# Pooled attention with a routed feed-forward: the product for x one half later, the fetch of rows behind the next row sums, the totals ahead of the transposes

## The chip, the cores and the metric
The kernel runs on one core of one Trainium2 chip. The metric is the device time of one execution in microseconds, the median of several runs. A core has five engines that run their own instruction streams side by side and wait for each other by semaphores: TensorE (PE, matrix products), VectorE (DVE), ScalarE (ACT), GpSimd (POOL) and SyncE (SP), which here only issues DMAs. Times within a profile count from the start of the profiled execution.

## The reference
Two blocks, one behind the other, on float32 data (8 batches, 8 heads, 1152 positions, head size 64).

```
q_pool = q.reshape(B, H, S // 2, 2, D).mean(axis=3)        # 576 queries
scores = (q_pool @ k.transpose) / sqrt(D)
attn   = softmax(scores)                                   # exps / (sum + 1e-9)
x      = (attn @ v) -> (B, 576, 512)                       # heads side by side

gate   = x @ w_gate                                        # one score per row
for each batch: top = the 128 rows with the largest gate
    ye      = relu(x[top] @ w1) @ w2                       # 512 -> 1024 -> 512
    out[top] = x[top] + sigmoid(gate[top]) * ye
the other rows of out are x
```

The softmax is taken without the maximum, since the inputs are small; a second version of the kernel behind a test at the end covers other inputs and is not run here.

## The kernel before
**Tiling.** Two heads make a *pair*, and there are 4 pairs in a batch, 32 in all. The 576 queries of a pair are split in two *halves* of 288, so the main loop of `run` has 64 halves and one closing round. A half h with h even (s == 0) is the first of its pair.

**One round h of the loop.** TensorE computes `scores` of half h: nine chunks of 128 keys, each an own PSUM tile (L818), and ScalarE takes the exps of each chunk into `p` (L825). Then TensorE computes `weighted` of the half before, the product of exps and values (L836). ScalarE copies it from PSUM to `two` (L844), GpSimd adds its two halves to `av` (L846), VectorE transposes that in blocks to `avb` (L915). All PSUM tiles come from one pool of four; `p` has two buffers. The loop is in the order in which each engine executes; nothing moves instructions afterwards. What stands earlier in the text of a round stands earlier on its engine, and an instruction that waits holds all behind it on the same engine.

**Row sums.** `folded` (L857, L862, L872) adds up the exps: GpSimd adds chunks 0 to 2 to chunks 3 to 5 in three instructions (`acc`), VectorE folds both `acc` and chunks 6 to 8. For the two halves of a pair this gives `sum`. Two rounds later ScalarE brings the four blocks of partitions side by side (`groups`, L887), VectorE adds them (`total`, L893, in `added`), and in the next round ScalarE spreads the result over the partitions (`sums`, L902). `normalized` takes the reciprocal on VectorE (`rec`, L954), and GpSimd multiplies `avb` by it to get `x` (L956), which `stored` writes to DRAM by SyncE a round later (L968).

**Gate.** `multiplied` (GpSimd, `prod`, L925) and `gated` (VectorE, L979, L981) compute each row's gate score from `avb` and `rec`.

**The feed-forward of a batch** is a generator, `routed`. It is cut into pieces by `yield`; `units` runs each open batch's next piece. A piece marked "mid" runs between a round's scores and its weighted product, all others at the end of the round. The pieces in order: the gate scores go by way of DRAM to a row and to columns; VectorE ranks each row by counting (L1083 to L1102); the ranks go by DRAM to all partitions (`lines`); VectorE searches each slot's row number and its gate (`pick`, L1166); GpSimd adds the batch's offset to make `index` (L1175) and fetches 128 rows of x from DRAM by an indirect DMA (`xe`, L1183). In later rounds TensorE transposes these rows (L1197), multiplies by w1 (L1208) and by w2 (L1221), and GpSimd adds the result to the rows (L1245) and scatters them (L1246). The last three batches differ: batch 5's second product is kept for the end of the kernel, and batches 6 and 7 have only pieces for the end of a round or behind the loop. Batch 7 gets its scores spread by a product with `diag` (L1044, L1054).

**The order of a round** on the engines other than TensorE: exps; the four copies of `groups` (even h) or `sums` (odd h) on ScalarE; pieces marked mid; `gated`; `folded`; `multiplied`; for even h `prepare_pair` (GpSimd adds pairs of queries, `qp`, L732; VectorE transposes `kT`, L735, and `qT`, L739); `weighted` and `drained`; `total` for even h; `rec` and `x` for odd h; the other pieces.

Of the kernel before, what the change touches and what calls it, by code (L numbers as in the profile page):

```python
# [10 lines left out]
P = 128  # L11
BLK = 32

G = 3
F32 = mybir.dt.float32
# [519 lines left out]
class _Plain:  # L535
# [396 lines left out]
    def normalized(self, pair):  # L932

        nc, hp = self.nc, pair["hp"]
        tot = self.sums[:, pair["b"] * self.NPAIR + hp, :]
        if self.last_pair(pair):
            ps = self.banks()[:, 0, :]
            nc.tensor.matmul(
                ps[:, 0 : 2 * self.QB],
                lhsT=self.merge.rearrange("p g j -> p (g j)"),  # L940
                rhs=pair["sum"].rearrange("p j n -> p (j n)"),
                start=True,
                stop=True,
            )
            for j in range(2):
                rows = slice(j * self.D, (j + 1) * self.D)
                nc.scalar.activation(
                    tot[rows, :],
                    ps[rows, j * self.QB : (j + 1) * self.QB],
                    AF.Identity,  # L950
                    bias=self.tiny[rows, 0:1],
                )
        rec = pair["rec"] = self.small.tile([P, self.QB], F32, name="rec")
        nc.vector.reciprocal(rec[:, :], tot)  # L954
        x = self.work.tile([P, self.QB, BLK], F32, name="x")
        nc.gpsimd.tensor_tensor(  # L956
            out=x[:, :, :],
            in0=pair["avb"][:, :, :],
            in1=rec[:, :].unsqueeze(2).broadcast_to([P, self.QB, BLK]),
            op=ALU.mult,  # L960
        )
        pair["x"] = x

    def stored(self, pair):

# [7 lines left out]
    def gated(self, half):  # L973

        nc, pair, hb = self.nc, half["pair"], self.HB
        if half["s"] == 0:
            pair["red"] = self.small.tile([P, self.QB], F32, name="red")
        ns = slice(half["s"] * hb, (half["s"] + 1) * hb)
        nc.vector.tensor_reduce(pair["red"][:, ns], pair["prod"][:, ns, :], AX.X, ALU.add)  # L979
        if half["s"] == 1:  # L980
            nc.vector.tensor_tensor(  # L981
                out=pair["part"][:, pair["hp"], :],
                in0=pair["red"][:, :],
                in1=pair["rec"][:, :],
                op=ALU.mult,
            )
            if pair["hp"] == self.NPAIR - 1:
                unit = self.routed(pair["b"], pair["part"])
                at = next(unit) == "mid"
                self.routing.append([pair["b"], unit, at])  # L990

# [3 lines left out]
    def routed(self, b, part):  # L997


        nc, ffn, Sp, NT, NF = self.nc, self.ffn, self.Sp, self.NT, self.NF  # L1000
        tiles = [(t, P if t < NF else self.TAIL) for t in range(NT)]
        mid = "mid" if b < self.B - 2 else True
# [8 lines left out]
        if b < self.B - 1:  # L1011

            yield mid
            if b < self.B - 2:
                groups = self.side_by_side(line)
                yield True
                total = self.added(groups)
            else:
                total = self.small.tile([BLK, self.QB], F32, name="total")
# [117 lines left out]
        for s0, w in self.slots:  # L1137
# [3 lines left out]
            if b == self.B - 1:  # L1141

                nc.vector.tensor_tensor(
                    out=pick[:, :, 0:w],
                    in0=self.slot_f[:, s0 : s0 + w].unsqueeze(1).broadcast_to([P, NT, w]),
                    in1=rank[:, :].unsqueeze(2).broadcast_to([P, NT, w]),
                    op=ALU.is_equal,
                )
                yield True
                ps = self.banks()[:, 0, 0:2]  # L1150
                for t, rows in tiles:
                    nc.tensor.matmul(
                        ps[0:w, :],
                        lhsT=pick[0:rows, t, 0:w],
                        rhs=meta[0:rows, t, :],
                        start=(t == 0),
                        stop=(t == NT - 1),
                    )
                nc.scalar.copy(index[0:w, :], ps[0:w, 0:1])
                nc.scalar.copy(own_gate[0:w, :], ps[0:w, 1:2])  # L1160
            else:
                yield True

                found = self.small.tile([P, 1], F32, name="found_token")
                for of, to in ((self.token_line, found), (lines[:, :, 1, :], own_gate)):
                    nc.vector.scalar_tensor_tensor(  # L1166
                        out=pick.rearrange("p t i -> p (t i)").rearrange("p (i t) -> p i t", t=NT)[0:w],
                        in0=lines[0:w, :, 0, :],
                        scalar=self.token[0:w, s0 // P : s0 // P + 1],
                        in1=of[0:w, :, :],  # L1170
                        op0=ALU.is_equal,
                        op1=ALU.mult,
                        accum_out=to[0:w, :],
                    )
                nc.gpsimd.tensor_scalar(  # L1175
                    out=index[0:w, :],
                    in0=found[0:w, :],
                    scalar1=float(b * Sp),
                    scalar2=None,
                    op0=ALU.add,  # L1180
                )
            xe = ffn.tile([P, self.Dm], F32, name="xe")
            nc.gpsimd.indirect_dma_start(  # L1183
                out=xe[0:w, :],
# [3 lines left out]
                bounds_check=(b + 1) * Sp - 1,  # L1188
                oob_is_err=False,
            )  # L1190
            yield True
            yield mid

            xeT = ffn.tile([P, self.ND, P], F32, name="xeT")
# [95 lines left out]
        )  # L1290
        return count_i

    def units(self, mid):


        for entry in self.routing[::-1]:
            b, unit, at = entry
            if b in self.waiting or at != mid:
                continue
            end = next((mark for mark in unit if mark), None)  # L1300
            if end is None:
                self.routing.remove(entry)
            elif end == "hidden" and b == self.B - 3:
                self.waiting.add(b)
            entry[2] = end in ("mid", "hidden") and b < self.B - 2

    def run(self):
        nc = self.nc
# [13 lines left out]
        for h in range(n_halves + 1):  # L1322
            if h < n_halves:
                n, s = divmod(h, 2)
                if s == 0:
                    pair = upcoming
                    if pair["hp"] == 0:
                        part = self.ffn.tile([P, self.NPAIR, self.QB], F32, name="part")
                    pair["part"] = part
                else:  # L1330
                    loaded = None
                    if n + 2 < len(pairs):
                        loaded = self.load_pair(*pairs[n + 2])
                        self.load_values(loaded)
                    if n > 1:
                        self.stored(halves[h - 4]["pair"])
                if h > 1:
                    next(weights, None)
                half = {"pair": pair, "s": s}
                halves.append(half)  # L1340
                self.scores(half)
                if h > 1:

                    of = halves[h - 2 - s]["pair"]
                    if s == 0:
                        of["groups"] = self.side_by_side(of["sum"].rearrange("p j n -> p (j n)"))
                    else:
                        self.spread(of)
                self.units(mid=True)
                if h > 2:  # L1350
                    self.gated(halves[h - 3])
                self.folded(half)
                if h > 1:
                    self.multiplied(halves[h - 2])
                if s == 0 and loaded:
                    upcoming = loaded
                    self.prepare_pair(upcoming)
            else:
                self.stored(halves[h - 3]["pair"])
                self.gated(halves[h - 3])  # L1360
                self.multiplied(halves[h - 2])
                self.units(mid=True)
                self.units(mid=False)
            if h > 0:
                done = halves[h - 1]
                self.weighted(done)
                self.drained(done)
            if h == n_halves:
                self.multiplied(done)
                self.gated(halves[h - 2])  # L1370
            if 1 < h < n_halves and s == 0:
                done["pair"]["total"] = self.added(done["pair"]["groups"])
            if h == n_halves:
                self.normalized(done["pair"])
            elif h > 2 and s == 1:
                self.normalized(halves[h - 2]["pair"])
            if h < n_halves:
                self.units(mid=False)
        for _ in weights:
            pass  # L1380

# [90 lines left out]
```

## Time and profile before
The time is 708.08 us, the median of three runs (707.3 to 708.53). The profiled execution took 706.64 us, 704.8 of them between its first and last instruction.

| engine | busy us | share |
| --- | --- | --- |
| TensorE, products | 694.4 | 99% |
| VectorE | 496.5 | 70% |
| GpSimd | 485.1 | 69% |
| ScalarE | 444.5 | 63% |

| group | count | mean ns |
| --- | --- | --- |
| `acc`, GpSimd L857 | 192 | 1417 |
| `x`, GpSimd L956 | 32 | 1159 |
| `index`, GpSimd L1175 | 7 | 920 |
| fetch of `xe`, GpSimd L1183 | 8 | 1140 |
| fold, VectorE L862 | 128 | 1963 |
| `total`, VectorE L893 | 37 | 325 |
| search, VectorE L1166 | 14 | 873 |

How to read it: a row of a list of groups gives line, engine, operation, output<-inputs, shapes and count, then busy time and mean duration, then the idle time of the engine just ahead and who ended it. A line of the chain in order of time has its start, its length and what it is. A line of a timeline has start, length, engine, line, operation and count, and in brackets the idle time ahead of it with the instruction that ended it. A line of the list of waits says who waited for whom: the sum in us, how often, the longest. An engine that is not the bound may be idle without any loss.

### The profile page before, as it was taken

Reading aid. Unit: us, or ns where it says so; the run is one execution under the profiler, and the core shown is the slowest. Engines: PE = TensorE matmul, PEld = TensorE weight load, DVE = VectorE, ACT = ScalarE, POOL = GpSimd, SP = SyncE. Lnnn points to the kernel's source line nnn. Section 1 sums busy time; section 2 is a strip of 40 time slices with the busy share of each in tenths; the row PEclk is TensorE's granted clock in tenths of the full one; section 3 lists DMA queues with packets and bytes.
Section 4 is the critical chain, followed back from the end, with each engine's and each line's share of the span. In section 5 each row is a group of like instructions: output and inputs, shape, how many; then the busy total and the mean of one; then the engine's idle time right before and its main releaser. Section 6 shows DMA issues by size and latency. Waiting matters only on the chain.

```text
span 704.8 us, 23397 instructions
## 1 busy us (share of the span) xinstructions
PE 694.4 (99%) x9948; PEld 516.8 (73%) x9948; DVE 496.5 (70%) x793; ACT 444.5 (63%) x963; POOL 485.1 (69%) x452
## 2 busy tenths in 40 slices
PE   8999999999999999999999999999999999999996
PEld 5668899996758866688656887578775787766573
DVE  3877777996559965498754988559774697689540
ACT  6677778777547775477746776467754777477210
POOL 5877777868658695586955779467874877686520
PEclk9999999999999999999999999999999999999999
DMA  8888887858486483756928468382775728432200
GB/s 175 172 178 180 171 166 137 146 116 161 85 149 111 85 162 75 145 97 111 172 40 159 81 129 160 66 148 61 161 130 85 135 56 169 83 72 62 45 31 35
DMA packets 389490, 82.86 MB, mean 118 GB/s; under 512 B 376640, under 2 KB 376640, under 8 KB 389376
## 3 DMA queue, kind: packets, MB, share of 16 engines
q1 hardware_dynamic: 387872, 76.49, 58.1%
q0 software_dynamic: 1280, 4.20, 1.8%
q8 instruction: 80, 1.31, 0.8%
q10 hardware_dynamic: 224, 0.59, 0.3%
q14 instruction: 34, 0.28, 0.1%
HBM read 69.65 MB, written 11.59 MB: 115 GB/s over the span
## 4 chain that ended last, share of the span: by engine, by line
PE 89%; POOL 5%; issue 2%; DMA 1%; ACT 1%; DVE 1%; SPq 0%; POOLq 0%; DVEq 0%; ACTq 0%
PE ps L836 36%; PE ps L818 36%; PE ps L1208 8%; PE ps L1221 7%; POOL acc L857 2%; ACT p L825 1%; DMA kb<-in_k_dram 1%; DMA xe<-out_dram,index 1%; PE ps L1197 1%; POOL prod L925 1%; POOL x L956 0%; POOL av L846 0%; DVE fold L862 0%; POOL index L1175 0%; SPq L759 0%
## 5 line engine op out<-in xcount | busy, mean ns | idle before, releaser
L825 ACT ACTIVATE p<-ps 128x576 f32<-128x576 f32 x576 | 320.2, 695 | 1.7 <-PE ps L818 1.3
L818 PE MATMUL ps<-qT,kT 64*64 64x288 f32 x4608 | 295.2, 404 | 0.2 <-ACT p L825 0.2
L836 PE MATMUL ps<-p,v_sb 64*64 64x288 f32 x4608 | 294.6, 403 | 0.0
L857 POOL TENSOR_TENSOR acc<-p 128x576 f32<-128x576 f32 x192 | 266.3, 1417 | 15.4 <-ACT p L825 15.1
L836 PEld LDWEIGHTS ps<-p,v_sb 64*64 64x64 f32 x4608 | 215.5, 133 | 65.3 <-ACT p L825 9.2
L818 PEld LDWEIGHTS ps<-qT,kT 64*64 64x64 f32 x4608 | 208.0, 132 | 73.0 <-ACT p L825 15.4
L862 DVE TRANSPOSE_TENSOR_REDUCE fold<-p 128x54 f32<-128x1728 f32 x64 | 126.0, 1969 | 50.2 <-ACT p L825 50.2
L862 DVE TRANSPOSE_TENSOR_REDUCE fold<-acc 128x54 f32<-128x1728 f32 x64 | 125.3, 1957 | 46.0 <-POOL acc L857 45.8
L844 ACT COPY two<-ps 128x576 f32<-128x576 f32 x64 | 40.9, 639 | 156.9 <-PE ps L836 143.8
L846 POOL TENSOR_TENSOR av<-two 128x288 f32<-128x288 f32 x64 | 51.2, 800 | 96.5 <-ACT two L844 94.9
L915 DVE STREAM_TRANSPOSE avb<-av 128x288 f32<-128x288 f32 x64 | 29.4, 460 | 66.5 <-POOL av L846 66.5
L956 POOL TENSOR_TENSOR x<-avb,rec 128x576 f32<-128x576 f32 x32 | 37.1, 1159 | 40.3 <-DVE rec L954 27.9
L1208 PEld LDWEIGHTS ps<-xeT,w 128*128 128x128 f32 x512 | 57.8, 192 | 2.7 <-ACT p L825 2.6
L1208 PE MATMUL ps<-xeT,w 128*128 128x128 f32 x512 | 59.3, 277 | 0.0
L1221 PE MATMUL ps<-w,hT 128*128 128x512 f32 x128 | 57.3, 598 | 0.0
L925 POOL TENSOR_TENSOR prod<-avb,w_gate 128x288 f32<-128x288 f32 x64 | 51.5, 805 | 0.6 <-DVE avb L915 0.6
L902 ACT ACTIVATE sums<-total,tiny 32x18 f32<-32x18 f32 x124 | 38.1, 308 | 15.9 <-DVE total L893 14.2
L732 POOL TENSOR_TENSOR qp<-qb 128x576 f32<-128x576 f32 x31 | 43.8, 1414 | 2.2 <-DMA qb<-in_q_dram 2.2
L1221 PEld LDWEIGHTS ps<-w,hT 128*128 128x128 f32 x128 | 23.6, 190 | 28.1 <-issue 25.8
L735 DVE STREAM_TRANSPOSE kT<-kb 128x1152 f32<-128x1152 f32 x31 | 42.5, 1370 | 0.0
L887 ACT COPY groups<-sum 32x36 f32<-32x36 f32 x124 | 27.1, 219 | 6.7 <-DVE sum L872 5.2
L981 DVE TENSOR_TENSOR part<-red,rec 128x18 f32<-128x18 f32 x32 | 27.0, 845 | 1.1
(95 smaller groups left out, 290.6 us busy)
## 6 DMA issues: line engine op xcount, KB each, us to landing
kb<-in_k_dram SPq DMA_DIRECT2D x124, 144.0 KB
qb<-in_q_dram SPq DMA_DIRECT2D x124, 144.0 KB
v_sb<-in_v_dram SPq DMA_DIRECT2D x124, 144.0 KB
out_dram<-x SPq DMA_DIRECT2D x128, 72.0 KB
lines<-row_rank SPq DMA_DIRECT2D x7, 640.0 KB
w<-in_moe_w_dram SPq DMA_DIRECT2D x8, 512.0 KB
sc_row<-row SPq DMA_DIRECT2D x7, 288.0 KB
acc<-in_q_dram ACTq DMA_DIRECT2D x2, 288.0 KB
```

Of the source, the lines that this page charges most:

```text
L732: nc.gpsimd.tensor_tensor(out=qp[:, :, :], in0=pair["q"][:, :, 0, :], in1=pair["q"][:, :, 1, :], op=ALU.add)
L735: nc.vector.transpose(kT.rearrange("p (c g i) -> p c g i", c=self.NC, i=BLK), pair["k"].rearrange("p (g c) d -> p c g d", c=self.NC),)
L818: nc.tensor.matmul(sc[keys, j, 0:n], lhsT=pair["kT"][rows, c * P + keys.start : c * P + keys.stop], rhs=pair["qT"][rows, qs], start=True, ...
L825: nc.scalar.activation(p[:, c // G, c % G, :, :], sc[:, :, 0:n], AF.Exp, scale=self.scale)
L836: nc.tensor.matmul(av[j * self.D : (j + 1) * self.D, e, 0:n], lhsT=half["pair"]["v"][keys, j, c, :], rhs=half["p"][keys, c // G, c % G, j, :],
L844: nc.scalar.copy(two[:, :, :], av[:, :, 0:n])
L846: nc.gpsimd.tensor_tensor(out=half["av"][:, :], in0=two[:, 0, :], in1=two[:, 1, :], op=ALU.add)
L857: nc.gpsimd.tensor_tensor(out=acc[:, u, :], in0=units[:, 0, u, :], in1=units[:, 1, u, :], op=ALU.add)
L862: nc.vector.tensor_reduce(fold[:, a, :], of.rearrange("p u (m d) -> p (u m) d", d=BLK), AX.X, ALU.add, apply_transpose=True,)
L925: self.nc.gpsimd.tensor_tensor(out=pair["prod"][:, ns, :], in0=pair["avb"][:, ns, :], in1=self.w_gate[:, hp : hp + 1, :].broadcast_to([P, ...
L1208: nc.tensor.matmul(pv[:, f, 0:w], lhsT=self.w1[:, c, (f0 + f) * P : (f0 + f + 1) * P], rhs=xeT[:, c, 0:w], start=(c == 0), stop=(c == self ...
L1221: nc.tensor.matmul(ps[0:w, 0 : self.Dm], lhsT=hT[:, f, 0:w], rhs=self.w2[:, f, :], start=(f == 0), stop=(f == self.NFC - 1),)
```

## The change
- **x one half later.** The product for `x` moves out of `normalized` into a function of its own, `divided`, which runs a round later, at the end of the even round. It is meant to keep GpSimd from waiting for the reciprocal, which VectorE finishes at the end of the odd round. The last two pairs keep their place.
- **The fetch behind the next row sums.** `index` is made by VectorE, right behind the search. For batches 0 to 5 the fetch becomes a piece with the mark "sums", which runs in the next round, just behind that round's `folded`. It is meant to keep GpSimd from waiting for the search ahead of the row sums.
- **The totals.** `total` moves from behind the weighted product to just behind `multiplied`, ahead of `prepare_pair`'s transposes on VectorE.
- **The closing round.** There the pieces of open batches run behind the last weighted product instead of ahead of it.

```diff
-        rec = pair["rec"] = self.small.tile([P, self.QB], F32, name="rec")
-        nc.vector.reciprocal(rec[:, :], tot)
-        x = self.work.tile([P, self.QB, BLK], F32, name="x")
-        nc.gpsimd.tensor_tensor(
+        pair["rec"] = self.small.tile([P, self.QB], F32, name="rec")
+        nc.vector.reciprocal(pair["rec"][:, :], tot)
+
+    def divided(self, pair):
+
+        x = pair["x"] = self.work.tile([P, self.QB, BLK], F32, name="x")
+        self.nc.gpsimd.tensor_tensor(
             out=x[:, :, :],
             in0=pair["avb"][:, :, :],
-            in1=rec[:, :].unsqueeze(2).broadcast_to([P, self.QB, BLK]),
+            in1=pair["rec"][:, :].unsqueeze(2).broadcast_to([P, self.QB, BLK]),
             op=ALU.mult,
         )
-        pair["x"] = x
...
-                nc.gpsimd.tensor_scalar(
+                nc.vector.tensor_scalar(
                     out=index[0:w, :],
                     in0=found[0:w, :],
...
+                if b < self.B - 2:
+
+                    yield "sums"
             xe = ffn.tile([P, self.Dm], F32, name="xe")
             nc.gpsimd.indirect_dma_start(
...
-            yield True
+            if b >= self.B - 2:
+                yield True
             yield mid
...
-            entry[2] = end in ("mid", "hidden") and b < self.B - 2
+            entry[2] = self.place(b, end)
+
+    def place(self, b, mark):
+        if mark in (True, None) or b >= self.B - 2:
+            return "end"
+        return "mid" if mark == "hidden" else mark
...
-                self.units(mid=True)
+                self.units("mid")
                 if h > 2:
                     self.gated(halves[h - 3])
                 self.folded(half)
+                self.units("sums")
                 if h > 1:
                     self.multiplied(halves[h - 2])
+                if 1 < h and s == 0:
+                    last = halves[h - 1]["pair"]
+                    last["total"] = self.added(last["groups"])
                 if s == 0 and loaded:
                     upcoming = loaded
                     self.prepare_pair(upcoming)
...
-                self.units(mid=True)
-                self.units(mid=False)
             if h > 0:
                 done = halves[h - 1]
                 self.weighted(done)
                 self.drained(done)
             if h == n_halves:
+                for at in ("mid", "sums", "end"):
+                    self.units(at)
                 self.multiplied(done)
                 self.gated(halves[h - 2])
-            if 1 < h < n_halves and s == 0:
-                done["pair"]["total"] = self.added(done["pair"]["groups"])
             if h == n_halves:
                 self.normalized(done["pair"])
+                self.divided(done["pair"])
             elif h > 2 and s == 1:
                 self.normalized(halves[h - 2]["pair"])
+
+            if h == n_halves - 1:
+                self.divided(halves[h - 2]["pair"])
+            elif 3 < h < n_halves and s == 0:
+                self.divided(halves[h - 3]["pair"])
             if h < n_halves:
-                self.units(mid=False)
+                self.units("end")
```

More of the change, by code (lines that the diff above doesn't have):

```diff
@@ L988, in gated @@
                 unit = self.routed(pair["b"], pair["part"])
-                at = next(unit) == "mid"
-                self.routing.append([pair["b"], unit, at])
+                self.routing.append([pair["b"], unit, self.place(pair["b"], next(unit))])
     def banks(self):
@@ L1291, in outside, with units @@
         return count_i
-    def units(self, mid):
+    def units(self, at):
         for entry in self.routing[::-1]:
-            b, unit, at = entry
-            if b in self.waiting or at != mid:
+            b, unit, place = entry
+            if b in self.waiting or place != at:
                 continue
```

## The prediction
> **What bounds the kernel now.** I read the page's busy shares first:
> ```profile
> PE 694.4 (99%) x9948; PEld 516.8 (73%) x9948; DVE 496.5 (70%) x793; ACT 444.5 (63%) x963; POOL 485.1 (69%) x452
> ```
> TensorE is busy 694.4 of 704.8 us. No product is removed, so all there is to win lies in its holes. Of the 10.4 us without a product 2.1 lie before the first scores and 6.6 behind the last product (698.2), both outside the change; 1.7 are in between. Busy time is a record of starts, so TensorE can also lose time inside it. Next I read the chain of work in order of time, around the feed-forward of batch 2 (half 34 begins at 333.32):
> ```profile
> 328.94 4.38 PE ps L836 x72
> 333.32 4.62 PE ps L818 x72
> 337.94 0.59 PE ps L1197 x4
> 338.53 4.52 PE ps L836 x72
> 343.05 4.37 PE ps L818 x72
> 347.42 7.34 PE ps L1208 x64
> ```
> A half's scores (L818) take 4.37 us everywhere, except in the half whose scores are followed by the transposes of the fetched rows (L1197). From the start of these scores to the transposes, the six batches 0 to 5 take 4.47, 4.55, 4.62, 5.05, 4.61 and 4.98 us. Less 4.37 each, that is 0.10 + 0.18 + 0.25 + 0.68 + 0.24 + 0.61 = **2.06 us**, the only loss that repeats. The timeline of GpSimd and of ScalarE tells why; first GpSimd:
> ```profile
> 316.71 0.80 POOL L846 TENSOR_TENSOR av<-two 128x288 f32<-128x288 f32 x1 [1.52 <-ACT two L844]
> 319.63 1.16 POOL L956 TENSOR_TENSOR x<-avb,rec 128x576 f32<-128x576 f32 x1 [2.12 <-DVE rec L954]
> 321.09 4.14 POOL L857 TENSOR_TENSOR acc<-p 128x576 f32<-128x576 f32 x3
> 327.33 0.79 POOL L846 TENSOR_TENSOR av<-two 128x288 f32<-128x288 f32 x1
> 331.08 0.92 POOL L1175 TENSOR_SCALAR index<-found_token 128x1 int32<-128x1 f32 x1 [2.97 <-DVE pick L1166]
> 332.28 1.13 POOL L1183 DMA_INDIRECT xe<-out_dram,index  x1 [0.28 <-POOL index L1175]
> 333.44 4.14 POOL L857 TENSOR_TENSOR acc<-p 128x576 f32<-128x576 f32 x3
> ```
> x waits 2.12 for the reciprocals, so the row sums (acc) of half 32 begin late, and av at 327.33 instead of just behind its input (ScalarE's copy `two` ended at 325.31). Then GpSimd waits 2.97 for the search of the rows on VectorE, and only then fetches; the fetch lands at 337.33, against the transposes at 337.94. The row sums of half 33 come last. On ScalarE:
> ```profile
> 333.81 0.64 ACT L844 COPY two<-ps 128x576 f32<-128x576 f32 x1 [2.31 <-PE ps L818]
> ```
> TensorE's product was done at 333.32, by its record, but the copy starts at 333.81, elsewhere 0.1 us after it. In batches 0, 1, 2, 4 and 5 this signal comes 0.1 to 0.4 us after the fetch instruction has ended (here 333.41), so I read it as held up while GpSimd writes the fetch's descriptors. The exps then start late, a PSUM tile comes free late, and the transposes wait. In batch 3 the fetch started a microsecond later (419.02) and landed at 423.90, just ahead of the transposes at 424.04. The list of waits gives the sums over the run:
> ```profile
> POOL x L956 <- DVE rec L954: 27.9, 17, 3.2
> POOL index L1175 <- DVE pick L1166: 20.2, 7, 3.0
> ACT sums L902 <- DVE total L893: 14.2, 7, 2.8
> ```
> None of the three is time of TensorE by itself: they are what the change goes at. Last, the end of TensorE's timeline:
> ```profile
> 648.00 4.59 PE L836 MATMUL ps<-p,v_sb 64*64 64x288 f32 x72
> 653.20 0.63 PE L1197 MATMUL ps<-ident,xe 128*128 128x128 f32 x4 [0.61 <-DMA xe<-out_dram,index]
> 653.76 4.59 PE L836 MATMUL ps<-p,v_sb 64*64 64x288 f32 x72
> 658.53 5.40 PE L1221 MATMUL ps<-w,hT 128*128 128x512 f32 x12
> 664.28 1.21 PE L1054 MATMUL ps<-diag,ones 128*128 128x288 f32 x4 [0.35 <-DVE rank_parts L1076]
> ```
> Two plain holes: 0.61 us for batch 6's fetched rows and 0.35 for `diag` (its signal is counted with the memset behind it).
>
> **What the Trainium skill says.** "Perfetto Trace Analysis", the section on the per-instruction lifecycle: a matmul's end in the profile is an estimate, and the end of a DMA that GpSimd issues is when its descriptors are written, not when data lands. The trace agrees: the product estimated to end at 333.32 was signalled near 333.75, and the fetch that "ends" at 333.41 landed at 337.33. "DMA: Bandwidth & Descriptors", section "Anatomy of one DMA — SWDGE (gpsimd) path": about 2.0 us plus bytes/436e3, which for 128 rows of 2 KB would be an estimate of 2.6 us. Here they took 3.4 to 5.8 us from the start of the instruction, beside the loads, so I use the trace. "GPSIMD Engine Reference", section "Engine selection": elementwise work is better on VectorE. The trace agrees for the index: 0.92 us on GpSimd for one column, where VectorE's tensor_scalar of one element (L1283) takes 0.14.
>
> **The change part by part.** I carry the times of batch 2 through.
>
> (1) x later. At the end of half 32 GpSimd no longer waits for the reciprocals: after av (to 317.5) it has only the small gate op (0.24) ahead of the row sums. These need the exps of chunk 3 of the half; ScalarE started at 316.47 and takes 5.00 for nine, so chunk 3 is ready near 318.8. Three sums of 1.38: 318.8 to 322.9, where they ran 321.09 to 325.2. With prod 0.80 and qp 1.41 GpSimd is free at 325.1, av follows its input, 325.4 to 326.1, and x, now here, takes 1.16: 327.3. Its load per pair stays, but the even half carries 4.14 + 0.80 + 1.41 + 0.80 + 1.16 = 8.3 us of the 8.74 that TensorE gives a half, the odd one 5.7. It fits, without much room; what would be late is row sums, and p's two buffers give them another half.
>
> (2) Fetch behind the next row sums. The exps of half 33 start at 325.20, chunk 3 is ready at 327.5, so the sums run 327.5 to 331.65. The instruction starts near **331.75**, 0.5 us ahead of before, if the index is there.
>
> (3) Index on VectorE, total ahead of the transposes. VectorE loses two waits: 0.27 for the gate op and 0.85 for acc, in front of the fold at 325.26. The second search, which ended at 331.9, ends near 330.8. The index comes behind it: lower end 0.14 (L1283), upper end 0.92 as on GpSimd; I take 0.17, since VectorE's other ops of a few columns take 0.13 to 0.19. Ready at 331.0, or 331.7 at the upper end: no wait at either. The total costs the same 0.33 in its new place; its input, ScalarE's groups, has been ready 3 us. kT is finished 0.33 later, more than 8 us ahead of its scores. ScalarE's wait of 14.2 us over 7 places goes; behind it stand `two` and the next exps, which in these halves still waited for TensorE, so this is worth nothing by itself.
>
> (4) What TensorE gets. The fetch instruction now runs 331.75 to 332.9; with the 0.3 that the signal was held after it, 333.2, just before the signal of 333.32. The rows land 3.4 to 5.8 later, 335.2 to 337.6; the transposes want them at 333.32 + 4.37 = 337.69. So both causes of the 2.06 us go, narrowly. I count five sixths: **1.7 us**.
>
> (5) The end. Batch 6's transposes move behind the last weighted product: the hole of 0.61 is filled with 4.5 us of products. `diag` must come earlier too. GpSimd's sums of half 62 no longer stand behind x (638.85 to 640.0) and end near 642.4 instead of 644.44; VectorE's fold then has no wait (0.84), nor the 0.27 of the gate. The index comes at 648.2 and not 649.3, the fetch starts at 648.4 and not 649.57, and the last row sums, fold, sum, rec, x, prod and diag move with it, by 1.2 us, from 664.2 to 663.0. TensorE gets there at 664.28 - 0.35 - 0.61 = 663.3. Gain 0.61 + 0.35 = **0.96 us**. After that TensorE has work without a gap to the last product. Moving the scatters behind x (1.16 us) changes no wait of over 0.05 us.
>
> Sum: 1.7 + 0.96 = 2.7; 708.08 - 2.7 = **705.4 us**.
>
> **The rivals.** *Hidden anyway:* the fetch starts only 0.5 us earlier, the signal is still caught by it, and landings scatter by 2.4 us. Then only the end counts: 708.08 - 0.96 = 707.1, no measurable change. For it: the margins of step 4 are 0.1 us. Against: both only improve. *Slower, the fetch behind late sums:* the fetch is now queued behind three ops of 1.4 us that themselves wait for exps. If GpSimd runs 1.5 us later than in step 2, the rows land a microsecond after TensorE wants them, in six batches: 708.08 + 6 - 0.96 = 713; were the sums to end as late as before (337.6), it would be 6 x 4.8 = 29 us more, 736. Against: what made them late, the waits for rec and for the search, is what goes. *Slightly slower, GpSimd's even half:* 8.3 of 8.74 us leaves 0.4, and the feed-forward's add and scatter (1.28 + 1.05) come on top; if exps then wait for p by 0.3 us in 6 places, 708.08 + 1.8 - 0.96 = 708.9. Against: these stand in halves that the feed-forward's products lengthen by 7 us.
>
> **How the numbers follow.** Forecast 0.62, hidden 0.20, late fetch 0.11, full even half 0.07. The forecast's own spread is 703.9 (all 3.0 us, and about as much again as the timed runs lie above the profiled 706.64) to 706.6; with the hidden case and part of the slow ones the range is 703.9 to 708.4. Faster by over 0.2% (under 706.66): nearly all of the forecast and a little of the hidden case, 0.65. Slower by over 0.2%: 0.16. Within: 0.19.
>
> **What would show it.** Right: fetches start about 1.6 us ahead of the end of the product in front, with index in VectorE's rows at under 0.2 us; no wait of x for rec and of sums for total; L1197 4.4 us behind the start of its scores; no hole at 653; L1054 near one microsecond earlier, relative to the last scores. Wrong: L1197 waiting for the DMA of xe, or acc of the half before the transposes ending after their scores began.

## The result, and the profile after
The changed kernel takes **716.15 us**, the median of six runs (714.05 to 719.2), against 707.44 for the kernel before (705.75 to 708.53). The ratio is 1.0125, with a 95% interval of 1.0096 to 1.0153. It is slower, and outside the predicted range of 703.9 to 708.4.

The profiled execution spans 712.5 us, 7.6 more than before. The busy shares of its page:
```profile
PE 692.8 (97%) x9948; PEld 526.7 (74%) x9948; DVE 494.4 (69%) x800; ACT 443.2 (62%) x963; POOL 481.7 (68%) x445
```
Apart from TensorE's weight loads (PEld, 516.8 us before), no engine is busy for longer than before. TensorE has the same products and longer holes. What TensorE waited for, from the list of waits (sum, times, longest):
```profile
PE ps L1202 <- DMA xe<-out_dram,index: 5.5, 4, 1.8
PE ps L1202 <- ACT p L825: 1.5, 2, 0.8
PE ps L1055 <- DVE rank_parts L1077: 1.3, 1, 1.3
```
L1202 is the transposes of the fetched rows (L1197 before). They now wait for the rows themselves. Around batch 2, GpSimd's timeline; all times here lie 0.87 us later than before, since half 34 starts at 333.93 instead of 333.06:
```profile
319.77 4.15 POOL L857 TENSOR_TENSOR acc<-p 128x576 f32<-128x576 f32 x3 [1.07 <-ACT p L825]
...
327.01 1.16 POOL L959 TENSOR_TENSOR x<-avb,rec 128x576 f32<-128x576 f32 x1
328.50 4.74 POOL L857 TENSOR_TENSOR acc<-p 128x576 f32<-128x576 f32 x3 [0.34 <-ACT p L825]
334.27 1.13 POOL L1187 DMA_INDIRECT xe<-out_dram,index  x1 [1.03 <-DVE index L1176]
```
and VectorE's, with the two searches and the index:
```profile
330.62 1.35 DVE L1167 SCALAR_TENSOR_TENSOR pick<-lines,token,token_line 128x640 f32<-128x640 f32 x1
...
332.01 1.90 DVE L1167 SCALAR_TENSOR_TENSOR pick<-lines,token 128x640 f32<-128x640 f32 x1
...
333.85 0.14 DVE L1176 TENSOR_SCALAR index<-found_token 128x1 int32<-128x1 f32 x1
```
Before, VectorE's timeline had them at
```profile
330.13 0.86 DVE L1166 SCALAR_TENSOR_TENSOR pick<-lines,token,token_line 128x640 f32<-128x640 f32 x1
...
331.03 0.89 DVE L1166 SCALAR_TENSOR_TENSOR pick<-lines,token 128x640 f32<-128x640 f32 x1
```
while GpSimd stood waiting for them. Now they lie beside the row sums and take 1.35 and 1.90, and three sums that take 4.15 elsewhere take 4.74. GpSimd still waits for the index, 1.03 us, only behind the sums now. So the fetch starts later, not earlier. The start of the transposes in the six batches, counted from the start of their scores, both in TensorE's timeline (this gives some 0.2 us more than the chain of waits that the prediction counted in; 4.55 is the least that any run shows, so I take 4.55 to 4.58 for no hole; e6 and e13 are experiments told below):

| | b0 | b1 | b2 | b3 | b4 | b5 |
| --- | --- | --- | --- | --- | --- | --- |
| before | 4.68 | 4.74 | 4.81 | 5.33 | 4.80 | 5.22 |
| after | 5.38 | 5.38 | 6.42 | 6.17 | 5.11 | 6.36 |
| e6 | 4.57 | 4.56 | 4.56 | 4.56 | 4.56 | 4.56 |
| e13 | 4.57 | 4.56 | 4.56 | 4.58 | 4.56 | 5.41 |

From before to after these add up to 5.2 us. The end, in TensorE's timeline:
```profile
652.72 8.96 PE L836 MATMUL ps<-p,v_sb 64*64 64x288 f32 x144
661.61 0.66 PE L1202 MATMUL ps<-ident,xe 128*128 128x128 f32 x4
...
669.61 1.21 PE L1055 MATMUL ps<-diag,ones 128*128 128x288 f32 x4 [1.29 <-DVE rank_parts L1077]
```
The hole of 0.61 us at the transposes is filled, but the product with `diag` waits 1.29 instead of 0.35. It comes 21.25 us behind the start of the last scores, before 20.64: 0.6 us lost. Last, the program ends 8.76 us behind the start of VectorE's last operation on the fetched rows (`xe`), before 6.46: 2.3 us lost. The three terms, 5.2 + 0.6 + 2.3 = 8.1, less the 0.4 us by which the first scores start earlier in this profile (8.31 against 8.73), cover the 7.6.

The spread of the six runs goes with the granted TensorE clock: three with a mean of 0.996 or 0.997, the profiled one (714.2) among them, took 714.05 to 715.62 us, and three with 0.992 took 716.69 to 719.2.

### The profile page after: what moved, and what is told of

It is laid out like the page before. It is cut to its first block, busy times and chain, and to the rows that moved or that the text cites. A ratio compares the mean times of both kernels' runs of the same rounds, so it can differ in the third digit from the quotient of the medians.

```text
span 712.5 us, 23370 instructions
## 1 busy us (share of the span) xinstructions
PE 692.8 (97%) x9948; PEld 526.7 (74%) x9948; DVE 494.4 (69%) x800; ACT 443.2 (62%) x963; POOL 481.7 (68%) x445
## 4 chain that ended last, share of the span: by engine, by line
PE 65%; DVE 13%; DMA 7%; POOL 6%; issue 5%; ACT 3%; SPq 0%; POOLq 0%; DVEq 0%; ACTq 0%
PE ps L836 27%; PE ps L818 23%; PE ps L1213 8%; PE ps L1226 5%; DVE fold L862 5%; POOL acc L857 3%; DMA xe<-out_dram,index 3%; ACT p L825 2%; DMA lines<-row_rank 2%; DVE kT L735 1%; DVE tie L1103 1%; DVE cmp L1093 1%; DVE cmp L1084 1%; DMA row_rank<-both 1%; DVE pick L1167 1%
## 5 line engine op out<-in xcount | busy, mean ns | idle before, releaser
L818 PEld LDWEIGHTS ps<-qT,kT 64*64 64x64 f32 x4608 | 215.9, 133 | 63.4 <-ACT p L825 6.1
L1221 ACT ACTIVATE hT<-ps 128x512 f32<-128x512 f32 x16 | 9.6, 597 | 32.3 <-PE ps L1213 32.3
```

The source lines that it names most:

```text
L818: nc.tensor.matmul(sc[keys, j, 0:n], lhsT=pair["kT"][rows, c * P + keys.start : c * P + keys.stop], rhs=pair["qT"][rows, qs], start=True, ...
```

## The experiments
Two theories stood at the beginning. A: the loss is the fetch, which now waits for searches that lie beside the row sums. B: the loss is x later. The first four kernels took the change apart.

**e1: x later alone** (`divided` and its calls; everything else as before).
```diff
+            if h == n_halves - 1:
+                self.divided(halves[h - 2]["pair"])
+            elif 3 < h < n_halves and s == 0:
+                self.divided(halves[h - 3]["pair"])
```


> The kernel before with one part of the change alone: the product for x one half later. Theory A (the loss is the fetch, whose index waits for searches that now run beside GpSimd's row sums): the fetch keeps its old place, so GpSimd idles during the searches, which stay at 0.86 and 0.89 us; VectorE starts the ranking about 1 us later (x stands ahead of the scatter) but loses two waits of 0.27 and 0.85; the fetch starts 8.0 to 8.6 us after the start of the half in front and the time is 707 to 709 us. Theory B (x one half later is itself the loss, by a full even half on GpSimd and a late VectorE): fetch a microsecond or more later, the hole ahead of the transposes of the fetched rows like the changed kernel's, 712 us or more.


Measured: 721.49 us, ratio 1.021 (1.0187 to 1.0234). Slower than the whole change. The fetch is fine here, as theory A said: five of six transposes come at 4.55 to 4.57. The loss of 15 us lies elsewhere: five rounds with a feed-forward lose 1.6 to 1.8 us each, and ahead of the last halves another 4.4 and 2.3. (Of the 4.4, TensorE stands 4.1 us for `line`, which VectorE sums up from the gate products of batch 6; over the 2.3 the granted clock was 0.5, for 6.8 us that began inside that hole.) In the first of these places VectorE's timeline shows why:
```profile
170.75 10.43 DVE L983 TENSOR_TENSOR part<-red,rec 128x18 f32<-128x18 f32 x1
```
A product of 128x18 takes 0.18 us when nothing disturbs it; here it takes 10.43. Over the run the 32 of them take 70.1 us, 27.0 before. What runs beside it on GpSimd, from a start at 168.94:
```profile
168.94 4.13 POOL L857 TENSOR_TENSOR acc<-p 128x576 f32<-128x576 f32 x3
173.04 0.79 POOL L925 TENSOR_TENSOR prod<-avb,w_gate 128x288 f32<-128x288 f32 x1
...
177.03 4.11 POOL L857 TENSOR_TENSOR acc<-p 128x576 f32<-128x576 f32 x3
```
with no gap up to 181.14. The product ends at 181.18. Every product of over 0.2 us in this run ends 32 to 42 ns behind the end of one of GpSimd's operations. Behind it on VectorE stands the fold, and behind that the total; on ScalarE
```profile
188.23 1.27 ACT L902 ACTIVATE sums<-total,tiny 32x18 f32<-32x18 f32 x4 [9.65 <-DVE total L893]
```
waits for the total, with `hT` of the feed-forward queued behind it, and TensorE waits 1.29 us for `hT`. This is a third theory, called W (windows) below: **VectorE's operations with two SBUF inputs wait for gaps of GpSimd's two-input operations, and the waits that the change removes were those gaps.** In the kernel before, `x` waited for `rec`, and the product got in when `x` ended:
```profile
340.59 1.16 POOL L956 TENSOR_TENSOR x<-avb,rec 128x576 f32<-128x576 f32 x1 [1.50 <-DVE rec L954]
...
340.86 0.92 DVE L981 TENSOR_TENSOR part<-red,rec 128x18 f32<-128x18 f32 x1
```
The Trainium skill has the rule in "SBUF — State Buffer", section "SBUF: two separate sides": a pair of SBUF ports is shared by GpSimd and VectorE as an exclusive lock for the length of an instruction, taken on VectorE's side by operations with two SBUF inputs or in a mode with two ports. The prediction didn't use it. The trace agrees that one side waits, but the 10.43 us take in the ends of nine GpSimd instructions, not of one.

**e2: the fetch moved alone** (index by VectorE behind both searches, `yield "sums"`, `units("sums")`).


> The kernel before with the other main part alone: index by VectorE behind both searches and the fetch behind the next row sums; x stays where it was. Theory A: the searches run beside the row sums and take 1.3 and 1.9 us as in the changed kernel, the index comes 9 us or later after the start of the half in front (before: 7.7), the fetch at 9.1 to 9.6, TensorE waits 1 to 2 us more at the transposes of each of batches 0 to 5: 712 to 716 us. Theory B: without the late x the index is early enough and the time is 706 to 709 us.


Measured: 718.48 us, ratio 1.0151 (1.0111 to 1.0191). Theory A holds for this part: the searches take 1.33 and 1.76 in the mean, the index is ready 9.2 us from the start of the half in front (before 7.7), and TensorE waits 11.0 us for fetched rows in 7 places. The time lies above the range of A (712 to 716); behind two of the holes (2.19 and 2.24 us) the granted clock was 0.5 for 3.4 us, which I estimate at 1.7 us more for each.

**e3: the change with the fetch at its old place.**
```diff
-                if b < self.B - 2:
-                    yield "sums"
...
-            if b >= self.B - 2:
-                yield True
+            yield True
```


> The changed kernel with the fetch back in its old place, at the end of the round and so ahead of the next row sums; index still by VectorE behind both searches, x late, totals early, closing round changed. Theory A: GpSimd idles for the index, the searches take 0.86 to 0.89 again, the index is there 8.0 us after the start of the half in front or a little earlier, the fetch at 8.0 to 8.2: body as before, 706 to 709 us, and up to 2.4 us more if the long closing of the changed kernel is there too. Theory B: no better than the changed kernel, 713 us or more.


Measured: 714.84 us, ratio 1.0123 (1.0098 to 1.0148), no better than the change, where A had expected 709 us at most, or 2.4 more with the long closing. The index is ready at 7.3 us in five batches, as A said, and four of the six holes at the transposes close; in batch 4 TensorE waits 1.5 us for the rows, in batch 5 0.7 for exps. `part` is back at 10.4 us (71.3 for all 32). The five rounds that lost 1.6 to 1.8 us in e1 lose nothing here (`total` stands earlier; that this is why was not tried), but behind the last long product (6.31 us) TensorE waits 3.7 us for `line`, and the granted clock is 0.5 for 3.4 us right behind that. In the changed kernel `part` takes 0.92 at most. There GpSimd paused for the index 5.1 us ahead of it, and in five of six batches again, by 0.1 to 0.3 us, 2.1 us ahead of it; in e1 and e3 GpSimd's last pause lies 8.6 us or more ahead. So the two losses hide each other in part, and A alone was not enough.

**e4: the change with the index between the two searches.**
```diff
-                nc.vector.tensor_scalar(out=index[0:w, :], in0=found[0:w, :], ...)
+                    if to is found:
+                        nc.vector.tensor_scalar(out=index[0:w, :], in0=found[0:w, :], ...)
```


> The changed kernel with the index made between the two searches, as it needs only the first one. Theory A: the index comes 1.9 us earlier, at 6.9 us after the start of the half in front; the fetch then waits only for the row sums, which end at 7.5 to 8.1, and starts at 7.7 to 8.2 instead of 9.1: most of the 5.2 us of hole ahead of the transposes go, 709 to 712 us (with the long closing 2.4 us more than without). Theory B: the index isn't what counts, 714 us or more.


Measured: 711.3 us, ratio 1.0078 (1.0051 to 1.0105). As A expected: the index needs only the first search, and in the change it is queued behind both, where before GpSimd made it beside the second. By the ratios that place costs (1.0125 - 1.0078) x 707 = 3.3 us, give or take 2.8 by the two intervals; in the profiles the six transposes come 4.4 us earlier in sum.

**e5: totals early and the new closing alone**, with x, index and fetch as before.


> The kernel before with only two parts of the change: totals in front of the transposes, and batch 6's transposes behind the last weighted product; x, the fetch and GpSimd's index as before. Theory W (windows: VectorE's operations with two inputs from SBUF run only in gaps of GpSimd's two-input operations; the loss of the change comes from the waits of GpSimd that x later and the moved fetch take away): GpSimd keeps its waits for rec and for the search here, so nothing is lost: 705.0 to 706.5, and searches stay at 0.86 and 0.89. Rival (the totals in front of the transposes delay VectorE's fold, or the new closing costs what the profile of after showed, 2.3 us behind the last fetched rows): 707.5 to 709.


Measured: 707.55 us, ratio 0.9998 (0.9988 to 1.0007). Neither gain nor loss, above the range that W gave (705.0 to 706.5). The longer closing that the rival named isn't there (6.4 us). The hole at the transposes is filled, and `diag` waits 1.29 instead of 0.35; it still comes 20.64 us behind the last scores. The chain of batch 7's gate scores sets that point, so the 0.61 us turned into a new wait.

**e6: the kernel before, with the index by VectorE between its searches** (the edit of e4, applied to the kernel before).


> The kernel before with one thing changed: the index is computed by VectorE, between its two searches, not by GpSimd behind the first. The fetch stays in front of the row sums. Theory W: index 0.14 instead of 0.92 us, so the fetch starts about 0.9 us earlier (7.0 instead of 7.96 us after the start of the half in front), the fetched rows' transposes come at 4.4 to 4.6 us from the start of their scores, and the part of 2.06 us that the prediction gave to this step comes: 704.0 to 705.5. The second search now lies beside row sums and takes 1.3 to 1.9 instead of 0.89, which nothing waits for. Rival (transposes are hidden anyway, or the earlier sums take from VectorE what the earlier fetch gives): 706 to 708.


Measured: 704.44 us, ratio 0.996 (0.9945 to 0.9976), faster than both kernels of the case. The row e6 of the table shows all six holes closed. The second search takes 0.88, not the 1.3 to 1.9 I expected: it runs beside the fetch instruction, which takes 1.52 us there in batch 2 (1.13 before).

**e9: e5 and e6 together.**


> The two kernels beside this one together: totals in front of the transposes and the new closing, and the index by VectorE between the searches, with x and the fetch where they were before. Theory W: the gains add up, 702.5 to 705, below both kernels of the case. Rival: the gain of one hides that of the other, 705 to 707.5.


Measured: 705.03 us, ratio 0.9967 (0.9957 to 0.9977). The gain of e6, and nothing on top: the rival's range, as e5 makes plain.

**e10: x later, with `part` on GpSimd.**
```diff
-            nc.vector.tensor_tensor(
+            nc.gpsimd.tensor_tensor(
                 out=pair["part"][:, pair["hp"], :],
```


> x later alone (721.49), with one more edit: the product of the 128x18 shares named part, with two inputs from SBUF, is done by GpSimd and not by VectorE. Theory W: the 15 us of x later came from this product (up to 10.4 us for 0.2 us of work, with the total and ScalarE's sums queued behind it), so most of it comes back: 706 to 713, and VectorE's part is gone from its slow operations. Rival (GpSimd's load in the even half, or the late x itself): GpSimd gets more work, so 721 or more.


Measured: 731.23 us, ratio 1.0336 (1.0293 to 1.0378). Missed. TensorE's waits for `hT` and for the gate line are gone as W says, but GpSimd now waits 81.9 us in 29 places for VectorE's `red`, with row sums and fetches queued behind it, and TensorE waits 15.3 us for fetched rows. The run moved the wait, so it doesn't decide between W and GpSimd's load.

**e11: x later, with a wait for `part` on GpSimd**, in all pairs.
```diff
+            seen = self.small.tile([P, 1], F32, name="seen")
+            nc.gpsimd.tensor_copy(seen[:, :], pair["part"][:, pair["hp"], 0:1])
```


> x later alone (721.49), with a wait added: directly behind VectorE's product part in the program, GpSimd copies one column of it (128x1), so that GpSimd's queue stops until the product is done. Theory W: the copy makes the gap that the product of two SBUF inputs needs; part takes at most 1 us everywhere (up to 10.4 us without the copy), the total and ScalarE's sums queued behind it come in time, the 1.6 us at five feed-forwards and the 4.4 + 2.3 us ahead of batch 6's last halves go: 706 to 711, though GpSimd has more instructions and one more wait. Rival (the even half on GpSimd is too full with x in it, and part is only late because its input is): an added wait makes it worse, 721 or more.


Measured: 733.81 us, ratio 1.0398 (1.0347 to 1.0449). Missed as well, for the same reason: the 32 products take 6.9 us in all, but GpSimd waits 88.6 us in 30 places, and TensorE 15.4 us for fetched rows.

**e12: the same copy, only for the last pair of a batch** (`if pair["hp"] == self.NPAIR - 1:`), where the ten-microsecond products were.


> x later alone (721.49) with the added copy of one column of part on GpSimd, but only for the last head pair of a batch, whose product was the one that took 6.3 to 10.4 us. So GpSimd stops in 8 places and not in 30, and in none of the halves with a fetch. Theory W: part of the last pair takes 0.2 to 0.9 us, the 1.6 to 1.8 us at five feed-forwards and the 4.4 + 2.3 us ahead of the last halves go, and the fetched rows' transposes stay on time as with x later alone: 704.5 to 709. Rival (the late x, not this product, is what costs): 716 to 722.


Measured: **706.05 us**, ratio 0.9973 (0.9964 to 0.9983). One copy of a column, with a wait, in each batch takes the ratio from 1.021 to 0.9973, that is 16.8 us off. The place shown for e1, on GpSimd
```profile
169.56 0.18 POOL L991 COPY seen<-part 128x1 f32<-128x1 f32 x1 [2.00 <-DVE part L983]
```
and on VectorE:
```profile
169.32 0.18 DVE L983 TENSOR_TENSOR part<-red,rec 128x18 f32<-128x18 f32 x1
```
GpSimd stands for 2.0 us, and the product takes 0.18 instead of 10.43. GpSimd's load is that of e1 and a little more, so B in the form "x makes GpSimd's half too full" is out, and W holds for x later. With the gap given back, x later is 1.9 us faster than the kernel before: five of the six transposes come at 4.55 to 4.57.

**m1: the disputed cost by itself.** Short operations of VectorE beside eight of GpSimd, in six stages A to F; nothing of the reference is computed.


> The disputed cost by itself; the whole computation of the reference is left out. Six stages, each with short operations of VectorE beside eight of GpSimd of 128x576: A, GpSimd adds two SBUF tiles, back to back (8 x 1.4 us); B, GpSimd scales one tile; C, as A, but each add waits for ScalarE first; D, as A, but VectorE's product has one input in PSUM; E, as A, with a wide product of VectorE (128x576) ahead of the narrow ones; F, GpSimd idle. VectorE's one-input scale of 128x18 and two-input product of 128x18. Theory W: in A the first product waits until the last add has ended (8 to 10 us), where the scales take 0.1; in B, C and F it takes under 1.5; in D 0.2; in E the wide product takes up to 10 us. Rival (the product was slow in the kernel for another reason, such as its input): 0.2 us in all stages.


VectorE's groups (busy us, mean ns; the last letter of the output is the stage):
```profile
L39 DVE TENSOR_SCALAR oneA<-u 128x18 f32<-128x18 f32 x9 | 5.7, 698 | 0.0
...
L37 DVE TENSOR_TENSOR twoA<-u,w 128x18 f32<-128x18 f32 x2 | 2.7, 1374 | 0.0
...
L39 DVE TENSOR_SCALAR oneF<-u 128x18 f32<-128x18 f32 x9 | 0.9, 170 | 0.0
...
L37 DVE TENSOR_TENSOR twoB<-u,w 128x18 f32<-128x18 f32 x2 | 0.6, 281 | 0.0
L37 DVE TENSOR_TENSOR twoF<-u,w 128x18 f32<-128x18 f32 x2 | 0.3, 172 | 0.0
...
L37 DVE TENSOR_TENSOR twoD<-u,pw 128x18 f32<-128x18 f32 x1 | 0.2, 160 | 0.0
```
and GpSimd's eight adds in stages A and E:
```profile
4.88 10.94 POOL L54 TENSOR_TENSOR big<-a,b 128x576 f32<-128x576 f32 x8
...
52.70 11.45 POOL L54 TENSOR_TENSOR big<-a,b 128x576 f32<-128x576 f32 x8
```
The product takes 0.17 us with GpSimd idle (F), 1.37 beside its adds (A) and 0.16 beside them with one input in PSUM (D). So for the product it is the two SBUF inputs that wait, and for GpSimd's two-input operations: beside its one-input scales (B) it took 0.17 and 0.40. But VectorE's one-input scale waits too (0.70 in the mean in A, 0.17 in F), which I hadn't expected: W names too few operations. The wide product (128x576) took 1.95 beside the adds and 0.75 alone, as the searches are stretched beside row sums. GpSimd waits in turn: the one add of E behind the wide product took 1.90 instead of 1.40, as sums do in the changed kernel. In stage C the adds ran without a gap after all, so C says nothing. One part of my expectation failed: here a product waits for the end of *one* add and then gets in, not for the last of eight.

**e7: the change with 24 memsets more on GpSimd at the start**, for the closing.


> The changed kernel with 24 memsets of one column more on GpSimd at the start of the program, which changes nothing but the count of GpSimd's instructions (658 to 682, as in the kernel before). Theory (the 2.3 us more behind the last fetched rows come from where GpSimd's instruction stream happens to be fetched at its closing): the end follows the last operation on the fetched rows by 6.4 us as before, not 8.76, and the time falls from 716.2 to about 714. Rival (the closing is longer for the work itself): 8.8 and 716.


Measured: 718.38 us, ratio 1.0156 (1.013 to 1.0182). The closing went from 8.76 to 6.35 us as expected, but the time did not fall: in the profile the fetched rows landed 0.3 to 1.1 us later, counted from the half in front, for a reason I haven't found, and two of the holes at the transposes were followed by a granted clock of 0.5 for 3.4 us (windows of TensorE around the one at 344.1; the columns are PE, PEld, DVE, ACT and POOL busy, then the granted clock, DMA share and GB/s):
```profile
344.10:351.00 6.90, 6.86 (x80) 4.19 (x84) 5.59 (x6) 0.59 (x1) 2.39 (x3) 0.75 0.77 121
351.00:357.00 6.00, 6.00 (x87) 4.17 (x80) 1.14 (x3) 5.86 (x12) 4.84 (x5) 1.00 0.82 157
```

**e13 and e14: the change with the fetch at its old place and the copy of e12; in e14 also the index between the searches.**


> The changed kernel with the fetch back in front of the row sums (714.84 by itself) and the copy on GpSimd behind part of the last head pair. What is left of the change: x later, totals early, index on VectorE behind both searches, the closing. Theory W: the ten-microsecond products go, the fetch is on time, so all of the loss goes but the longer closing behind the last fetched rows (2.3 us, if it appears): 704 to 707. Rival (what the changed kernel loses with its fetch at the old place has another source too): 709 or more.

> The kernel beside this one with the index computed between the two searches. The fetch then starts about 0.9 us earlier, as in the kernel before with that edit alone. If the fetch at the old place is still short of time: 1 to 2 us below the kernel beside it, 702.5 to 705. If the transposes are already without a hole: the same as it.


Measured: e13 706.58 us, ratio 0.9984 (0.9975 to 0.9993); e14 705.17 us, ratio 0.9964 (0.995 to 0.9978). So with the gap for `part` and the fetch back in front, nothing of the loss is left. e13 against e3 is the copy alone: 1.0123 to 0.9984, or 9.8 us. Some 2.1 of them are the closing, which is at 6.6 us in both (8.7 in e3) and goes with GpSimd's instruction count (last section). On top of the index's place, x later and the early totals bring nothing: e14 is level with e6.

## Why the prediction was wrong
**Step 3 failed first.** It took the searches at the 0.86 and 0.89 us of the trace before, as if a duration belonged to the operation. They were measured with GpSimd standing still for them, and the change puts row sums beside them. Counted from the start of half 34, step 3's second search should have ended at 330.8; it ended at 333.85 + 0.08 - 0.87 = 333.1. Of these 2.3 us, 1.5 are the longer searches ((1.35 + 1.90) - (0.86 + 0.89)), the rest a later start of the first: VectorE was busy without a gap ahead of it, and only 0.4 of the expected 1.1 us came. The index itself took 0.14 us, the step's lower end. That step also laid it behind both searches without asking which it needs: e4 puts 3.3 us on that, and e6 shows that the same index between the searches makes the whole gain that steps 2 to 4 hoped for.

**Steps 2 and 4 fell with it.** The sums began at 327.6 in the clock of before (predicted 327.5) and ended at 332.4, 0.7 late through the stretched sum. The fetch started at 333.4, 1.65 us behind the 331.75 of step 2. The rows took 5.9 us to land, just beyond the 3.4 to 5.8 that was used. They were late in four batches; in the other two TensorE waited 0.7 to 0.8 us each for exps. Whether TensorE's signal is held up while GpSimd writes descriptors, on which step 4 leaned, no run tests by itself. The 1.7 us to be won became 5.2 us lost. The rival "the fetch behind late sums" named the right place and nearly the right size (713), but the wrong cause: the sums were 0.7 us late, but it was the index that the fetch waited for.

**Step 1 was right in its times and wrong in its verdict.** The first sums began at 318.9 (predicted 318.8), av at 325.4 (predicted 325.4). But it treated the 27.9 us that x waited for rec as time free to be given away. e1 and e12 show that they were what VectorE's `part` ran in. By itself x later costs 15 us; that the changed kernel kept pauses in which `part` got in was luck, as the prediction didn't look for them. With the gap given back (e12) x later wins 1.9 us, near the 1.7 of step 4, and e6 wins the same holes by another way; the two don't add up (e14).

**Step 5:** the hole of 0.61 us was filled and came back as a wait of `diag`; e5 puts the gain of this part at nothing instead of 0.96 us. `diag` did not come earlier: in batch 6 the index was ready 0.6 us later, not 1.2 earlier. That goes with x later: in the ten kernels that have it `diag` comes 21.1 us or more behind the start of the last scores, in the five without it 20.6 or less. The 2.3 us behind the last rows were in no step: the prediction had set the 6.6 us behind the last product outside the change.

What would show it wrong was named rightly: the transposes waiting for the DMA of `xe`.

## What to carry to other kernels
A wait of an engine may be the window in which another engine works. Before you remove waits of GpSimd, list VectorE's operations that lie in them, and take none of their durations over to a place where GpSimd runs two-input operations. Put what a DMA's address needs directly behind the operation that makes it, ahead of anything else on that queue.

## What the runs showed of the hardware that was not expected
- **Passed over, again and again.** In m1 a product got in at the next end of an add. In e1 five products of the last pair passed over eight ends of GpSimd operations each (10.4 us), and one over five (6.3), until GpSimd paused or ran a memset; others in the same run got in at the next end (0.28 to 0.92). What decides that is open. In the 14 kernels that have `part` on VectorE, the 308 that waited for one end only had begun at most 5.1 us behind GpSimd's last pause of over 0.06 us; the twelve that passed over five or eight ends had begun 8.6 us or more behind it, and one in e7 that passed over two, 4.9. But in m1 a product got in at the next end 8.8 us into an unbroken row of adds, so this is not the whole rule.
- **A hole can cost more than its length.** Over all these profiles TensorE has 17 holes of 2.08 to 4.11 us between start-up and closing. In or right behind 12 of them, from 2.10 us on, the granted clock fell to 0.5 for 3.4 us (6.8 at the longest hole); I estimate the loss of such a stretch at up to 1.7 us, half of the 3.4. It fell at no shorter hole, the longest of these 2.00 us. The Trainium skill, "TensorE: Matmul & The Clock Gate", section "Part 1: The HAM clock gate", puts the idle time that lowers the clock at about 3.4 us; here holes from 2.1 us on did it.
- **The closing.** From the start of the last operation on `xe` to the end it took 8.7 to 8.8 us in the three kernels with 658 instructions on GpSimd in the trace, waits and branches counted (after, e3, e4), and 6.35 to 6.9 in the others, with 651, 659, 666, 682 or 688. e7, which adds only memsets, moved it from 8.76 to 6.35. In the trace the difference is one place: GpSimd's last long drain starts 2.2 to 2.4 us behind the semaphore in front of it in these three, 0.08 in all others. It goes with the instruction count; why was not tried.
